# Half of x and grad_out turned by DMA, gate sums on VectorE, and quartered group loads in a gated spectral and dense kernel

## The chip, the cores and the metric

The kernel runs on one core of one Trainium2 chip. A core has a matrix engine (TensorE, PE in the profile, with its weight loads as PEld), a vector engine (VectorE, DVE), a scalar engine (ScalarE, ACT), a general engine (GpSimd, POOL) and a sync engine (SyncE, SP). In this kernel SP and POOL hand out the DMA transfers, each in the order of its own queue. SBUF is the memory on the core that the engines read, PSUM is where TensorE writes, DRAM is the chip's main memory. The metric is the time on the device from the first to the last instruction, in microseconds (us).

## The reference

The function mixes two branches with a gate per row and is differentiated; the kernel computes the output and the eight gradients.

```python
x = A_x                                          # (1, 2048, 1024), bf16
g = sigmoid((x * gate_w).sum(-1, keepdims=True))
a = irfft2(rfft2(x) * (w_r + 1j * w_i))          # spectral branch
h = relu(x_B @ w1 + b1) ** 2                     # dense branch, F = 3584
b = h @ w2 + b2
out = g * a + (1 - g) * b
# and the vector-Jacobian product with grad_out for
# A_x, w_r, w_i, w1, b1, w2, b2, gate_w
```

In the reference's `_fwd_reference` the dense branch reads the same `x` as the spectral branch.

## The kernel before

The 2048 rows are cut into 16 tiles of 128 rows (`NT`), the 1024 columns into 8 chunks of 128 (`DC`), and F = 3584 into 28 chunks of 128 (`FC`). Everything is written as Python generators, and `spread` (L948) interleaves a main generator with a side one, some side steps to each main step. A planner in the framework then sets the order on each engine from the order of the code and the data; each engine runs its own list in order.

The stages are:

- The opening (L976 to L1029). `rows_of_x` loads x tiles into `xsrc` buffers (four of them), `rows_of_grad` loads grad_out tiles into `dbn`. `turn_x` and `turn_grad` turn a tile on PE: eight 128x128 transposes into PSUM by `turn_tile` (L571 to L576), and one copy into `xT` (by ScalarE) or `dbT` (by VectorE). `gate` (L584) computes the gate of four tiles: 32 matmuls with one column each, two sigmoids into `omg` (1 - g) and `gcol` (g), and a scaling of the four `dbn` tiles by `omg` on VectorE (L597). A turn of a `dbn` tile comes after its scaling.
- `mlp_in` (L635) does the dense branch's first half. `hidden` (`forth`) multiplies two chunks of `w1` by `xT` (`ph`, eight matmuls of 512 columns) and takes relu and square on ScalarE; `grads` (`back_`) multiplies `w2T` by `dbT` (`pd`, eight matmuls) and ends in `dhT` on VectorE (L661). `ph` and `pd` share two PSUM banks. A step covers 512 rows (`s`, four row tiles) and one chunk of F. For the first two pairs of chunks (`fp` 0 and 1, here called a block of F each) the steps go through `s` from 0 to 3, forth for both, back for both; the other 12 run one by one. `load_w1` loads a `w1` pair, and `load_w2` loads `w2T` by two DMAs that transpose. `finish` stores `h2T` and `dhT` to DRAM through POOL.
- The side work of that stage is the first Fourier stage of x and then of grad_out (`first_stage_of_x`, `first_stage_of_grad`): `folds` on VectorE, `row_stage` and `first_columns` on PE, and stores of `z` through POOL. Its input tiles are the `src` buffers, loaded through SP.
- `mlp_grads` (L743) computes the gradients of w2 and w1 in 14 jobs. Each job needs a group: 512 columns of `h2T` or `dhT`, brought back from DRAM by four transposing DMAs on SP (`group`, L749). There are two group buffers, and the next job's group is asked for at the start of a job. The side work is the middle of the Fourier work (`fft_mid`) and its last part (`fft_out`), which also loads `r` tiles through SP and stores through POOL.
- `mlp_out` (L827) computes the output and the gradient of x.

Of the kernel before, what the change touches and what calls it, by code (L numbers as in the profile page):

```python
# [10 lines left out]
P = 128  # L11
BF16 = mybir.dt.bfloat16
# [113 lines left out]
def kernel(  # L126
# [66 lines left out]
    gwcol = cols("gwcol", [DC], BF16)  # L193
# [279 lines left out]
    def fft_out():  # L473
# [64 lines left out]
        load(0), load(1)  # L538
        folded(0)
        for n in range(len(tiles) + 1):  # L540
            if n < len(tiles):
                rows_back(n)
                yield
            if n > 0:
                columns_back(n - 1)
            if n + 2 < len(tiles):
                load(n + 2)
            if n + 1 < len(tiles):
                folded(n + 1)
            yield  # L550
# [15 lines left out]
    def source(i, view, earlier=None, tag="src"):  # L566
        src = f1.tile([P, D], BF16, name=tag, tag=tag, bufs=4)
        after(ld(out=src[:], in_=view[i]), earlier)
        return src
# [8 lines left out]
    def vectors(vrow):  # L578
        vps = tps.tile([P, FC + DC], BF16, name="vps", tag="tr", bufs=2)
        nc.tensor.transpose(vps[:], vrow[:], identb[: FC + DC, : FC + DC])  # L580
        nc.vector.tensor_copy(out=b1col[:], in_=vps[:, 0:FC])
        nc.vector.tensor_copy(out=gwcol[:], in_=vps[:, FC : FC + DC])

    def gate(i0):  # L584

        c_ = slice(i0, i0 + 4)
        pg = tps.tile([P, 4], FP32, name="pg", tag="tr", bufs=2)
        for i in range(i0, i0 + 4):
            for dc in range(DC):
                mm(  # L590
                    pg[:, i - i0 : i - i0 + 1], lhsT=xT[:, dc, of_tile(i)], rhs=gwcol[:, dc : dc + 1],
                    start=(dc == 0), stop=(dc == DC - 1), skip_group_check=True,
                )
        nc.scalar.activation(omg[:, c_], pg[:], ACT.Sigmoid, scale=-1.0)
        nc.scalar.activation(gcol[:, c_], pg[:], ACT.Sigmoid)
        for i in range(i0, i0 + 4):
            nc.vector.tensor_scalar(out=dbn[:, i, :], in0=dbn[:, i, :], scalar1=omg[:, i : i + 1], scalar2=None, op0=ALU.mult)  # L597

    def first_stage_of_x():
        f, ft = {0: folds(f1, xs[0], later["last"])}, {}  # L600
        for i in range(NT + 1):
            if i + 3 < NT:
                xs[i + 3] = source(i + 3, x_perm, later["last"])
            if i < NT:
                ft[i] = row_stage(f1, f[i], kf[:], later["last"])
                yield
            if i > 0:
                first_columns(f1, cf, 0, i - 1, ft[i - 1], later["last"])
            if i + 1 < NT:
                f[i + 1] = folds(f1, xs[i + 1], later["last"])  # L610
            yield
# [23 lines left out]
    def mlp_in():  # L635
# [38 lines left out]
        wide = lambda n_: wb.tile([P, 2, 2 * SW], BF16, name=n_, tag=n_, bufs=4)  # L674
        rows_ = lambda s: slice(s * SW, (s + 1) * SW)

        def load_w1(fp):
            w1[fp] = wb.tile([P, DC, PW], BF16, name="w1g", tag="w1g", bufs=3)
            ld(out=w1[fp][:], in_=w1v[:, :, fp * PW : (fp + 1) * PW])
# [6 lines left out]
        def back_(fp, s, c):  # L686
            fg, pr = divmod(fp, NPR)
            step = 2 * s + c
            last = grads(2 * fp + c, s, rows_(s), rTs.pop((fp, s, c)), dh[fp, s // 2][:, c, rows_(s % 2)])
            later["last"] = last  # L690
            if 8 * pr + step == 3:
                later["blocks"] = last
                if 0 < fg < FG - 1:
                    load_w2(fg + 1, last)
            if c == 1 and s % 2 == 1:
                finish(fp, s // 2)
# [14 lines left out]
        for s in range(4):  # L711
            for what in (forth, back_):
                for fp in range(2):
                    for c in range(2):
                        what(fp, s, c)
                        yield
            if s == 2:
                load_w1(2)
                load_w2(1, later["last"])
        for fp in range(2, FC // 2):  # L720
            if fp + 1 < FC // 2:
                load_w1(fp + 1)
            for s in range(4):
                for c in range(2):
                    forth(fp, s, c)
                    back_(fp, s, c)
                    yield
# [15 lines left out]
    def mlp_grads():  # L743
# [5 lines left out]
        def group(scr, fg, earlier=None):  # L749
            t_ = strm.tile([P, NT, FGW], BF16, name="grp", tag="strm", bufs=2)  # L750
            v_ = scr[:].rearrange("c p s -> (c p) s")[fg * FGW : (fg + 1) * FGW, :]
            for k in range(4):
                after(turned(t_[:, 4 * k : 4 * (k + 1), :], v_[:, 4 * k * P : 4 * (k + 1) * P]), earlier)
            return t_
# [3 lines left out]
        nxt = group(*jobs[0], later["blocks"])  # L758
# [3 lines left out]
        for n, (scr, fg) in enumerate(jobs):  # L762
            cur = nxt
            if n + 1 == len(jobs):
                later["block"] = blocks(h2T_scr)(0)
            else:
                nxt = group(*jobs[n + 1], later["blocks"])
# [12 lines left out]
            if scr is h2T_scr:  # L780
                for fb_ in range(FGC):
                    wo = wb.tile([P, D], BF16, name="wo2", tag="wo2", bufs=2)
                    for hf in range(NH):
# [6 lines left out]
                        last = nc.scalar.copy(out=wo[:, hf * H : (hf + 1) * H], in_=pw[:])  # L790
                        if n in (2, 3):
# [6 lines left out]
            else:  # L798
                for d_ in range(DC):
# [7 lines left out]
                    nc.scalar.copy(out=wo[:], in_=pw[:])  # L807
# [168 lines left out]
    zeros = f1.tile([P, H], BF16, name="zeros", tag="zeros")  # L976
    nc.vector.memset(zeros[:], 0.0)
    pz = tps.tile([P, H], FP32, name="pz", tag="tr", bufs=2)
    for _ in range(7):
        mm(pz[:], lhsT=zeros[:, 0:P], rhs=zeros[:], start=True, stop=True)  # L980
# [3 lines left out]
    vrow = f1.tile([FC + DC, P], BF16, name="vrow", tag="vrow")  # L984
    st(out=vrow[0:FC, :], in_=B_b1.rearrange("(fc p) -> fc p", p=P))
    st(out=vrow[FC : FC + DC, :], in_=gate_w.rearrange("(fc p) -> fc p", p=P))
# [3 lines left out]
    for i in range(4):  # L990
        turn_x(i)
    vectors(vrow)
# [4 lines left out]
    stage = None  # L997
    for k in range(NT // 4):
        i = 4 * k
        if k + 1 < NT // 4:  # L1000
            rows_of_grad(k + 1)
        next(units)
        turn_grad(i), turn_grad(i + 1)
        next(units)
        turn_grad(i + 2)
        next(units)
        turn_grad(i + 3)
        next(units)
        if stage:
            next(stage)  # L1010
        next(units)
        if k + 1 < NT // 4:
            turn_x(i + 4), turn_x(i + 5)
        next(units)
        if k + 1 < NT // 4:
            turn_x(i + 6), turn_x(i + 7)
        next(units)
        if k + 1 < NT // 4:
            gate(4 * (k + 1))
        if k + 2 < NT // 4:  # L1020
            rows_of_x(k + 2)
        if k == 0:
            for n in range(3):
                xs[n] = source(n, x_perm)
            stage = first_stage_of_x()
        next(stage)
        next(units)
        next(stage)
# [6 lines left out]
    n = 0  # L1035
    mixed = spread(units, first, 0.9)
    while n < 72:
        next(mixed)
        n += 1
# [13 lines left out]
    todo = 1 + 12 * (S2 // 2) + 2 * NT  # L1053
# [41 lines left out]
```

## Time and profile before

The times of the kernel before:

| what | value |
|---|---|
| median of 3 timed runs | 1309.12 us |
| lowest, highest | 1309.04 us, 1311.78 us |
| span of the profiled execution | 1308.4 us |
| DMA traffic over the span | 234.20 MB, 179 GB/s in the mean |

The profile is one execution. A line of the groups reads: code line, engine, operation, what is written `<-` what is read, shapes, count, then busy time and mean duration of one, then the idle time of the engine just before them and what ended most of it. A line of the timeline reads: start, duration, engine, line, operation, and a count where neighbours are merged. A line of the waits reads: who waited `<-` for whom, total, times, longest. In windows over the span PE's share stands close to full from 12 us on:

| window, us | PE busy | DVE busy | ACT busy | DMA share |
|---|---|---|---|---|
| 0 to 12 | 8.20 | 0.59 | 6.31 | 0.85 |
| 12 to 60 | 47.14 | 25.61 | 29.11 | 0.81 |
| 60 to 444 | 381.62 | 146.20 | 207.34 | 0.52 |
| 444 to 850 | 402.33 | 266.62 | 125.39 | 0.85 |
| 850 to 900 | 47.35 | 21.87 | 21.93 | 0.55 |
| 900 to 1309 | 402.50 | 221.72 | 34.45 | 0.66 |

The DMA share is the mean busy share of 16 DMA engines in the window.

### The profile page before, as it was taken

To read this page: it belongs to the slowest core of one execution; us is meant where nothing else is said; L and a number is where in the kernel's file an instruction comes from. 1 tells how busy PE (TensorE), PEld (TensorE's weight loads), DVE (VectorE), ACT (ScalarE), POOL (GpSimd) and SP (SyncE) were. 2 spreads that over 40 slices of the span, in tenths; PEclk is the share of its full clock that TensorE was granted. 3 is DMA by queue.
4 is the path that set the end of the run, shared out by engine and by line. 5 is a ranking of instruction groups with operands and counts; after the bars stand their busy time and mean duration, and the time that the engine had idled before them with its cause. 6 is when DMAs were issued, how large, how long until landed. Compare 5 with 4: busy or idle time off the path is not lost. (4 is left out here: it accounts for less than half of the span.)

```text
span 1308.4 us, 18055 instructions
## 1 busy us (share of the span) xinstructions
PE 1289.1 (99%) x6922; PEld 627.4 (48%) x7057; DVE 682.6 (52%) x1516; ACT 424.5 (32%) x722; POOL 191.3 (15%) x337
## 2 busy tenths in 40 slices
PE   8999999999999999999999999999999999999998
PEld 5555544555544444444444445554444444444443
DVE  3554424444312495677766772445767678722222
ACT  5656655666533323323233333342111111000000
POOL 0111111111110122122113221221000001000000
PEclk9999999999999999999999999999999999999999
DMA  9566354554526688898797759956999986743440
GB/s 298 181 185 178 129 155 144 184 142 157 146 97 161 173 217 183 240 242 197 185 178 159 156 140 272 306 193 175 224 198 216 228 202 195 215 130 105 131 119 25
DMA packets 314280, 234.20 MB, mean 179 GB/s; under 512 B 183701, under 2 KB 263601, under 8 KB 314193
## 3 DMA queue, kind: packets, MB, share of 16 engines
q1 hardware_dynamic: 289552, 150.58, 48.7%
q0 software_dynamic: 24640, 82.46, 19.0%
q8 instruction: 55, 0.90, 0.3%
q14 instruction: 33, 0.26, 0.1%
HBM read 107.14 MB, written 81.81 MB: 144 GB/s over the span
## 5 line engine op out<-in xcount | busy, mean ns | idle before, releaser
L647 PE MATMUL ph<-xT,w1g 128*128 128x512 bf16 x862 | 217.0, 379 | 1.7
L657 PE MATMUL pd<-dbT,w2T 128*128 128x512 bf16 x879 | 209.9, 379 | 1.1
L802 PE MATMUL pw<-grp,res 128*128 128x512 bf16 x872 | 200.0, 379 | 1.9 <-ACT wo L807 0.7
L786 PE MATMUL pw<-dbn,grp 128*128 128x512 bf16 x875 | 199.6, 379 | 1.1
L872 PE MATMUL acc<-w,hblk 128*128 128x512 bf16 x875 | 195.7, 379 | 1.1
L661 DVE SCALAR_TENSOR_TENSOR dhT<-pd,rT 128x512 bf16<-128x512 f32 x112 | 77.4, 691 | 228.6 <-PE pd L657 170.2
L932 PE MATMUL accg<-w1Tr,hblk 128*128 128x512 bf16 x878 | 192.9, 379 | 0.9
L932 PEld LDWEIGHTS <-hblk 128*128 128x128 bf16 x896 | 87.4, 98 | 105.7 <-issue 0.9
L657 PEld LDWEIGHTS <-w2T 128*128 128x128 bf16 x896 | 87.2, 98 | 102.5
L786 PEld LDWEIGHTS <-grp 128*128 128x128 bf16 x896 | 86.8, 98 | 103.2 <-issue 0.9
L872 PEld LDWEIGHTS <-hblk 128*128 128x128 bf16 x896 | 86.3, 98 | 98.5
L802 PEld LDWEIGHTS <-res 128*128 128x128 bf16 x896 | 86.2, 98 | 98.6 <-issue 1.0
L647 PEld LDWEIGHTS <-w1g 128*128 128x128 bf16 x896 | 84.7, 98 | 89.1
L649 ACT ACTIVATE rT<-ph,b1col 128x512 bf16<-128x512 f32 x112 | 76.9, 686 | 111.2 <-PE ph L647 107.9
L936 DVE TENSOR_TENSOR gxo<-accg,g 128x512 bf16<-128x512 f32 x32 | 22.1, 690 | 120.9 <-PE accg L932 120.9
L790 ACT CAST wo<-pw 128x512 bf16<-128x512 f32 x56 | 32.7, 584 | 142.1 <-PE pw L786 136.0
L807 ACT CAST wo<-pw 128x512 bf16<-128x512 f32 x56 | 32.8, 585 | 136.6 <-PE pw L802 78.4
L650 ACT ACTIVATE h2T<-rT 128x512 bf16<-128x512 bf16 x112 | 70.5, 629 | 2.5
L505 ACT CAST rt<-pki 128x1024 f16<-128x1024 f32 x32 | 32.6, 1018 | 98.1 <-PE pki L503 98.0
L331 DVE TENSOR_TENSOR x<-px,common 128x1024 f16<-128x1024 f32 x32 | 38.8, 1220 | 40.7 <-ACT common L328 40.7
L532 POOL DMA_DIRECT2D ax_scr<-yo x32 | 17.3, 540 | 235.4 <-DVE yo L531 223.9
L873 DVE SCALAR_TENSOR_TENSOR ot<-acc,omg,af 128x512 bf16<-128x512 f32 x32 | 23.9, 747 | 52.8 <-PE acc L872 52.7
(182 smaller groups left out, 1300.8 us busy)
## 6 DMA issues: line engine op xcount, KB each, us to landing
h2T_scr<-h2T POOLq DMA_DIRECT2D x28, 512.0 KB, 4.2
dhT_scr<-dhT POOLq DMA_DIRECT2D x28, 512.0 KB, 4.9
hblk<-h2T_scr SPq DMA_DIRECT2D x8, 1792.0 KB, 8.6
hblk<-dhT_scr SPq DMA_DIRECT2D x8, 1792.0 KB, 8.5
z_scr<-u POOLq DMA_DIRECT2D x32, 256.0 KB, 2.9
z<-z_scr SPq DMA_DIRECT2D x16, 512.0 KB, 4.9
y_scr<-pc POOLq DMA_DIRECT2D x16, 512.0 KB, 7.5
r<-y_scr SPq DMA_DIRECT2D x32, 256.0 KB, 3.8
```

The source lines that it names most:

```text
L331: V(out=x[:, j, :, 0:H].rearrange("p c (i g) -> p c i g", g=4), in0=px[:].rearrange("p c (g i) -> p c i g", g=4), in1=common[:].rearrange( ...
L647: mm(ph[:], lhsT=w1g[:, dc, fc % 2 * P : (fc % 2 + 1) * P], rhs=xT[:, dc, ss], start=(dc == 0), stop=(dc == DC - 1))
L649: nc.scalar.activation(rT[:], ph[:], ACT.Relu, bias=b1col[:, fc : fc + 1])
L650: nc.scalar.activation(h2T, rT[:], ACT.Square)
L657: mm(pd[:], lhsT=w_[:, ec, fc % FGC * P : (fc % FGC + 1) * P], rhs=dbT[:, ec, ss], start=(ec == 0), stop=(ec == DC - 1),)
L661: return STT(out=dhT, in0=pd[:], scalar=2.0, in1=rT[:], op0=ALU.mult, op1=ALU.mult, accum_out=gb1part[:, fc, sb : sb + 1],)
L786: mm(pw[:], lhsT=cur[:, t, fb_ * P : (fb_ + 1) * P], rhs=dbn[:, t, hf * H : (hf + 1) * H], start=(t == 0), stop=(t == NT - 1),)
L790: last = nc.scalar.copy(out=wo[:, hf * H : (hf + 1) * H], in_=pw[:])
L802: mm(pw[:], lhsT=xr[t][:, d_ * P : (d_ + 1) * P], rhs=cur[:, t, :], start=(t == 0), stop=(t == NT - 1),)
L807: nc.scalar.copy(out=wo[:], in_=pw[:])
L872: turn["PE"] = mm(acc[:], lhsT=cur[:, fc, t2 * P : (t2 + 1) * P], rhs=w2[:, fc, cs], start=(fc == 0), stop=(fc == FC - 1))
L932: turn["PE"] = mm(acc[:], lhsT=cur[:, fc, t2 * P : (t2 + 1) * P], rhs=w1T[:, fc, cs], start=(fc == 0), stop=(fc == FC - 1),)
```

## The change

It has five parts.

1. The gate's dot products move from PE to VectorE. `gate_dot(i)` multiplies a row tile of x by `gate_w`, which is broadcast to all 128 partitions by a load through POOL, and sums along the row into `gdot`. `gate` takes its sigmoids from there. The gate's part of `vectors` goes.
2. x and grad_out tiles 8 to 15 are turned by transposing DMAs on SP, x from DRAM and grad_out from the scaled `dbn` in SBUF. Tiles 0 to 7 are still turned on PE. All 16 row tiles of x are still loaded, for the gate.
3. The opening of `mlp_in` takes four blocks of F (`fp` 0 to 3) where it took two: both halves of the blocks with `s` 0 and 1 first, then with 2 and 3. `w1` gets four buffers instead of three, `dhT` three instead of four, and the loads of `w1` and `w2T` move with this. The first Fourier stage of x starts later, and its loads go through POOL.
4. In `mlp_grads`, the four DMAs of a group are asked for one at a time, after four of the eight steps of a job.
5. Smaller edits: the warm-up of PE takes 25 matmuls of 128 columns instead of 7 of 512; a sigmoid of one column at the start loads ScalarE's table; `fft_out` has three more yields before its first steps, and `todo` counts them.

```diff
@@ fft_out @@
         load(0), load(1)
+        yield
+        yield
         folded(0)
+        yield
@@ opening helpers @@
+    def gate_dot(i):
+        junk = f1.tile([P, D], BF16, name="junk", tag="zeros")
+        nc.vector.tensor_tensor_reduce(
+            out=junk[:], in0=rows[i][:], in1=gw_bc[:], scale=1.0, scalar=0.0,
+            op0=ALU.mult, op1=ALU.add, accum_out=gdot[:, i : i + 1],
+        )
     def gate(i0):
         c_ = slice(i0, i0 + 4)
-        pg = tps.tile([P, 4], FP32, name="pg", tag="tr", bufs=2)
-        for i in range(i0, i0 + 4):
-            for dc in range(DC):
-                mm(
-                    pg[:, i - i0 : i - i0 + 1], lhsT=xT[:, dc, of_tile(i)], rhs=gwcol[:, dc : dc + 1],
-                    start=(dc == 0), stop=(dc == DC - 1), skip_group_check=True,
-                )
-        nc.scalar.activation(omg[:, c_], pg[:], ACT.Sigmoid, scale=-1.0)
-        nc.scalar.activation(gcol[:, c_], pg[:], ACT.Sigmoid)
+        nc.scalar.activation(omg[:, c_], gdot[:, c_], ACT.Sigmoid, scale=-1.0)
+        nc.scalar.activation(gcol[:, c_], gdot[:, c_], ACT.Sigmoid)
@@ first_stage_of_x @@
-                xs[i + 3] = source(i + 3, x_perm, later["last"])
+                xs[i + 3] = source(i + 3, x_perm, later["last"], load=st)
@@ mlp_in @@
-        wide = lambda n_: wb.tile([P, 2, 2 * SW], BF16, name=n_, tag=n_, bufs=4)
+        wide = lambda n_: wb.tile([P, 2, 2 * SW], BF16, name=n_, tag=n_, bufs=4 if n_ == "h2T" else 3)
-            w1[fp] = wb.tile([P, DC, PW], BF16, name="w1g", tag="w1g", bufs=3)
+            w1[fp] = wb.tile([P, DC, PW], BF16, name="w1g", tag="w1g", bufs=4)
-                if 0 < fg < FG - 1:
+                if 1 < fg < FG - 1:
                     load_w2(fg + 1, last)
-        for s in range(4):
+        parts = [(0, 0), (1, 0), (0, 2), (1, 2), (2, 0), (3, 0), (2, 2), (3, 2)]
+        for n, (s, fp0) in enumerate(parts):
+            if n == 1:
+                load_w1(2), load_w1(3)
+                load_w2(1, later["last"])
+            if n == 6:
+                load_w1(4)
+                load_w2(2, later["last"])
             for what in (forth, back_):
-                for fp in range(2):
+                for fp in (fp0, fp0 + 1):
                     for c in range(2):
                         what(fp, s, c)
                         yield
-            if s == 2:
-                load_w1(2)
-                load_w2(1, later["last"])
-        for fp in range(2, FC // 2):
+        for fp in range(4, FC // 2):
@@ mlp_grads @@
-            for k in range(4):
-                after(turned(t_[:, 4 * k : 4 * (k + 1), :], v_[:, 4 * k * P : 4 * (k + 1) * P]), earlier)
-            return t_
+            def quarter(k, earlier):
+                after(turned(t_[:, 4 * k : 4 * (k + 1), :], v_[:, 4 * k * P : 4 * (k + 1) * P]), earlier)
+            return t_, quarter
...
+                nxt, quarter = group(*jobs[n + 1])
+                if n == 0:
+                    for k in range(4):
+                        quarter(k, later["blocks"])
+            quarters = {0: 0, 1: 1, 3: 2, 4: 3} if 0 < n < len(jobs) - 1 else {}
...
                         last = nc.scalar.copy(out=wo[:, hf * H : (hf + 1) * H], in_=pw[:])
+                        if 2 * fb_ + hf in quarters:
+                            quarter(quarters[2 * fb_ + hf], last)
...
+                    last = nc.scalar.copy(out=wo[:], in_=pw[:])
+                    if d_ in quarters:
+                        quarter(quarters[d_], last)
@@ the opening @@
-    for _ in range(7):
-        mm(pz[:], lhsT=zeros[:, 0:P], rhs=zeros[:], start=True, stop=True)
+    nc.scalar.activation(gdot[:, 0:1], zeros[:, 0:1], ACT.Sigmoid)
+    for _ in range(25):
+        mm(pz[:, 0:P], lhsT=zeros[:, 0:P], rhs=zeros[:, 0:P], start=True, stop=True)
...
+    gw_bc = f1.tile([P, D], BF16, name="gw_bc", tag="gw_bc")
+    st(out=gw_bc[:], in_=gate_w.partition_broadcast(P))
...
     for i in range(4):
+        gate_dot(i)
         turn_x(i)
...
+    for k in range(2):
...
+        gate_dot(i + 4), gate_dot(i + 5)
+        if k == 0:
             turn_x(i + 4), turn_x(i + 5)
...
+    rows_of_grad(3)
+    for i in range(8, 12):
+        turned(xT[:, :, of_tile(i)], x_perm[i])
+    for i in range(8, 12):
+        turned(dbT[:, :, of_tile(i)], dbn[:, i, :])
+    for n in range(3):
+        xs[n] = source(n, x_perm, later["last"], load=st)
+    stage = first_stage_of_x()
+    for n in range(4):
+        gate_dot(12 + n)
+        next(units)
+    gate(12)
+    for i in range(12, 16):
+        turned(xT[:, :, of_tile(i)], x_perm[i])
+    for i in range(12, 16):
+        turned(dbT[:, :, of_tile(i)], dbn[:, i, :])
...
-    mixed = spread(units, first, 0.9)
+    for _ in spread((next(units) for _ in range(36)), first, 0.5):
+        pass
+    for _ in spread((next(units) for _ in range(60)), first, 0.95):
+        pass
```

In the prediction a unit is one step of `mlp_in` that the opening takes from its generator: eight `ph` or eight `pd` matmuls while forth and back are apart.

## The prediction

> **What bounds the kernel now.** I read the page's busy shares first, then TensorE's (PE's) waits, then the groups by shape, then the timeline of the opening.
>
> ```profile
> PE 1289.1 (99%) x6922; PEld 627.4 (48%) x7057; DVE 682.6 (52%) x1516; ACT 424.5 (32%) x722; POOL 191.3 (15%) x337
> ...
> PE 34%; issue 0%; DVE 0%; ACT 0%
> ```
>
> PE is busy 99% of the span, and the chain that ended last is PE alone. A microsecond leaves the span only if PE does less, or waits less. Its waits, the longest first, are few:
>
> ```profile
> PE pui L282 <- ACT e L513: 2.3, 1, 2.3
> PE pt L575 <- DMA identb<-c_identb: 1.3, 1, 1.3
> PE pz L980 <- DVE zeros L977: 1.2, 1, 1.2
> PE pw L802 <- ACT wo L807: 0.7, 1, 0.7
> ```
>
> The second and third are the start of the kernel. The first and fourth fall together, near 847 and 853 us, while SP hands out a whole turned group (last fence below). So the waits that can be won add up to 3.0 us; the rest must come from PE's own work:
>
> ```profile
> L575 PE MATMUL pt<-identb,xsrc 128*128 128x128 bf16 x128 | 9.7, 236 | 1.6 <-DMA identb<-c_identb 1.3 <-ACT xT L576 0.2
> L575 PE MATMUL pt<-identb,dbn 128*128 128x128 bf16 x128 | 9.1, 219 | 0.0
> L590 PE MATMUL pg<-gwcol,xT 128*128 128x1 bf16 x128 | 3.8, 163 | 0.3 <-DVE gwcol L582 0.3
> ```
>
> The means (219 and 163 ns) are latencies of pipelined instructions, not prices. Prices come from distances between starts. The chain in order of time gives undisturbed runs:
>
> ```profile
> 857.52 0.45 PE pki L503 x8
> 857.96 3.45 PE pw L802 x16
> ```
>
> 16 wide matmuls take 3.45 us, so 8 take 1.725. The timeline of the opening then shows what stands between two such eights:
>
> ```profile
> 13.90 1.89 PE L647 MATMUL ph<-xT,w1g 128*128 128x512 bf16 x8
> ...
> 15.63 0.61 PE L575 MATMUL pt<-identb,dbn 128*128 128x128 bf16 x8
> ...
> 16.08 1.89 PE L647 MATMUL ph<-xT,w1g 128*128 128x512 bf16 x8
> ...
> 25.22 1.89 PE L657 MATMUL pd<-dbT,w2T 128*128 128x512 bf16 x7
> ...
> 26.94 0.94 PE L590 MATMUL pg<-gwcol,xT 128*128 128x1 bf16 x32
> ...
> 27.75 1.89 PE L657 MATMUL pd<-dbT,w2T 128*128 128x512 bf16 x8
> ```
>
> From 13.90 to 16.08 is 2.18: 1.725 plus 0.455 for one turned tile. From 25.22 to 27.75 is 2.53: 0.80 for one gate of 32 tiny matmuls.
>
> **What the Trainium skill says.** "VectorE: DVE Perf Modes", The three transpose paths: a 128x128 turn costs 390 ns on TensorE, 1309 ns by DMA. The trace has 0.455 us for eight on PE in a stream, far less. "Advanced Engine Details and Errata", X-Bar Transpose (TRN2): such DMAs run about as fast as ordinary ones. No turn of one tile is in this trace; the nearest is half a w2T load, 256 rows, which is two tiles. "DMA: Bandwidth & Descriptors", Issuing engines are not separate DMA queues: moving a load from SP to POOL saves only issue time. The trace shows nothing against it. "ScalarE: Activation LUTs", What ACT_TABLE_LOAD costs: about 1.28 us plus a drain; the trace has two loads of 1.28 us, at 0.72 and 10.83.
>
> **The change, part by part.**
>
> Turning. PE keeps x and grad_out tiles 0 to 7 and drops 8 to 15: 16 tiles x 0.455 = 7.3 us off PE. The 16 PSUM copies that go with them (ACT 1.0, DVE 0.69 each) were beside PE and are worth nothing.
>
> Gates. The later three gates leave PE: 3 x 0.80 = 2.4 us. The first one stood between the last turned tile and the first wide matmul (11.50). That matmul now needs only the last xT copy, which ended at 10.81; I put it at 11.1, so 0.4 less (bounds 0.7 less to 0.3 more, as w1g(0) shares the DMAs with the new 256 KB broadcast). The warm-up, the early sigmoid and its table load are over before identb lands at 5.7: nothing, hidden behind that load.
>
> Gate dots on DVE. The nearest row is the same operation with float32 input: L850, 128x1024, 1219 ns. I take 1.3 us with its accumulator read; 16 are 21 us on an engine that was 53% busy from 12 to 60 us. The price is not the work but the place. DVE runs in order, and in the built order the dots stand ahead of what PE waits for:
> - Dots 0 to 3 wait for the gate row's broadcast. Issued near 2.5, and with the cf load's 6.8 us to landing, that gives about 8.9; four dots and one b1col copy end at 14.4, the scaled first dbn tile is there at 15.3. PE has run two eights by 14.4: 0.9 us of wait. The first relu queues behind the two sigmoids, no more than that.
> - Dot 4 stands ahead of the copy of dbT tile 3, which the first pd needs. Tile 4's load leaves SP at 17.2 and landed 3.2 later, at 20.4; dot and copy end at 22.5, PE is ready at 21.1: 1.5.
> - Dots 6 to 9 stand ahead of the dhT reads that free the two ph/pd banks: 0.8, and 0.35 for a late dbT tile 7.
> - Dots 12 and 13 stand ahead of the first dhT of block (1,0), and their rows stand on SP behind w1(2), w1(3) and the two halves of w2T(1), which wait for DVE themselves (about 33.5). SP is then free near 38, rows land near 42 to 43; dots and dhT end at 45.3 where PE is ready at 44.1: 1.3, then three times 0.3.
> Sum: 0.9 + 1.5 + 0.8 + 0.35 + 1.3 + 0.9 = 5.75, say 6. Bounds: 1, if the loads land a microsecond or two sooner and DVE catches up; 13, if the w2T halves hold SP as long as the first pair did (10.16 us) and each late dot is passed on whole.
>
> Turned loads on SP.
>
> ```profile
> 6.93 10.16 SPq L166 DMA_TRANSPOSE w2T<-in_B_w_dram  x2
> 17.21 1.93 SPq L568 DMA_DIRECT2D xsrc<-in_A_x_dram  x4
> ...
> 70.44 3.83 SPq L166 DMA_TRANSPOSE w2T<-in_B_w_dram  x2
> ...
> 830.09 15.79 SPq L166 DMA_TRANSPOSE grp<-dhT_scr  x4
> ```
>
> A pair of halves, four tiles' worth, held SP 10.2 us while the DMAs were full and 3.8 when not, so a tile takes 1 to 2.5 us of SP; I take 1.5, 24 us for 16, from about 42 on. First need: xT 8 to 11 at unit 33, near 49 + 16 x 1.725 + some first-stage work = 78; the last (dbT 12 to 15) near 101. Hidden, with 59 us for 16 turns. The first-stage x loads go from SP to POOL's queue, past the h2T, dhT and z stores; POOL was 11% busy in the opening (3.4 of 48 us), so nothing. Four blocks of F instead of two give these turns their time; the same eights run in another order: nothing on PE. dhT with three buffers: the fourth tile in use comes 8 units (over 14 us) after the store of the first, which lands in 4.9: nothing.
>
> Quartered groups. SP no longer gives 15.8 us to one group while the r loads and stores wait; I take both waits near 850 as gone, 3.0 us (bounds 0 and 3.4). The last quarter is issued after five eighths of a job of some 33 us and landed in 6 (at most 13): hidden. The three extra yields only delay the first fold, off PE.
>
> **Sum**, against its own span: -7.3 - 2.4 - 0.4 - 3.0 + 6 = -7.1; 1308.4 to 1301.3. The three timed runs are 1309.04 to 1311.78, median 1309.12, 0.7 above the span: forecast 1302.
>
> **Rivals.**
> - The dots' waits are mostly taken up: +1 instead of +6, time 1297. For it: DVE has slack, and landings of 3 us were seen. Against: an order that can't be swapped at run time.
> - The waits grow to 13 or so, or the quarters win nothing beside them: 1309, no change to measure. For it: the DMAs were full from 2 to 40 us.
> - Slower: the one-tile turns, out of SBUF above all, are not half of a w2T half but cost SP a fixed time each. Place: SP between 42 us and unit 45. From 59 / 16 = 3.7 us each PE begins to wait. At 5 us, the last would be there at 42 + 80 = 122, 21 us late: 1302 + 21 = 1323. At the skill's 1309 ns for each of eight blocks in turn it would be worse. For it: no such turn in the trace. Against: w2T halves, two tiles each, ran at 1.9 us.
>
> **How the numbers follow.** Forecast 0.55, waits taken up 0.20, no change 0.12, late turns 0.13. The forecast's own range is 1298 to 1307 (waits 2 to 11). To hold 8 in 10 over all, I leave out most of the slow rival and some of the fast: 1295 to 1311. A difference under 0.2% (2.6 us) can't be told from none here. Faster: 0.55 x 0.95 + 0.20 = 0.72. Same: 0.03 + 0.10 = 0.13. Slower: the late turns and a little of the third case, 0.15.
>
> **What would show it.** PE's L575 groups at 64 + 64 and no L590; the PE busy sum down by about 10 at equal means; PE waits between 14 and 52 us, put down to DVE (dbT, dhT), summing to 4 to 8; no wait at 845 to 855. I am wrong if PE waits for DMA into xT or dbT after 75 us, if the opening's waits exceed 11, or if new PE waits for grp quarters appear between 445 and 850.

## The result, and the profile after

The changed kernel is slower: 1327.1 us in the median of four runs (1324.18 to 1329.72), against 1310.16 us for the kernel before beside it (1309.04 to 1311.78). The ratio is 1.0128, with a 95% interval of 1.0100 to 1.0155. The forecast was 1302 us, so the sign was wrong. The profiled execution has a span of 1322.4 us, 14.0 more than before; it is the fastest of the four, so some 3 us of the median are not in it.

The page's busy shares and its chain of waits, for the changed kernel:

```profile
PE 1284.0 (97%) x6686; PEld 619.4 (47%) x6819; DVE 699.0 (53%) x1539; ACT 414.1 (31%) x714; POOL 204.1 (15%) x353
...
PE 75%; issue 11%; DVE 6%; DMA 4%; POOL 3%; ACT 1%; SPq 0%; another core or an unknown queue 0%; POOLq 0%; DVEq 0%; ACTq 0%
```

TensorE (PE) is busy only 5 us less than before, although some 10 us of turns and gate sums left it. It now idles for 38 us instead of 19. The chain that ended last now goes back over the whole span, and a quarter of it isn't PE; before, it reached back over a third of the span, all of it PE. TensorE's waits in the changed kernel say where:

```profile
PE pw L820 <- DMA grp<-dhT_scr: 8.5, 2, 7.5
PE pd L659 <- DVE dhT L663: 5.0, 1, 5.0
...
PE pd L659 <- DVE dbT L579: 1.4, 1, 1.4
```

Two waits are large and new, and they lie in two different stages. The starts of the stages, read from the timeline as the first matmul of each, split the 14.0 us:

| start of | before | after | stage longer by |
|---|---|---|---|
| `mlp_grads`, jobs on `h2T` | 445.0 | 447.5 | 2.5 (up to here) |
| `mlp_grads`, jobs on `dhT` | 670.9 | 677.0 | 3.6 |
| `mlp_out` | 897.7 | 912.4 | 8.6 |
| end | 1308.4 | 1322.4 | -0.7 |

The prediction had -4.1 for the first row (all but the quarters) and -3.0 for the second and third. Both were wrong.

**The late quarter.** The timeline of SP's queue in one job on `dhT` of the changed kernel (the job ran from 805.4 to 837.3 us), with the wait of the next job on PE:

```profile
809.66 9.49 SPq L166 DMA_TRANSPOSE grp<-dhT_scr  x1
819.26 0.51 SPq L488 DMA_DIRECT2D r<-y_scr  x1
819.83 0.42 SPq L536 DMA_DIRECT2D w<-in_B_w_dram  x1
820.34 7.04 SPq L166 DMA_TRANSPOSE grp<-dhT_scr  x1
...
830.26 6.88 SPq L166 DMA_TRANSPOSE grp<-dhT_scr  x1
...
837.86 3.61 SPq L166 DMA_TRANSPOSE grp<-dhT_scr  x1
```
```profile
847.52 1.87 PE L820 MATMUL pw<-grp,res 128*128 128x512 bf16 x4 [7.55 <-DMA grp<-dhT_scr]
```

The last quarter of the group was due near 825.8, when ScalarE's copy of the fifth step ends. It is handed out at 837.86, after the job that should have hidden it has ended, and it lands 9.6 us later. The three quarters before it held SP 9.5, 7.0 and 6.9 us; the four together make 27.0. Before the change the whole group handed out at 830.09 held it 15.8. After the wait TensorE isn't at full speed; windows of the changed kernel (us, PE busy with its instructions, granted clock, DMA share, GB/s):

```profile
840.00:844.00 4.00, 0.00 (x0) 0.78 1.03 193
844.00:848.00 4.00, 0.48 (x2) 0.50 1.03 263
848.00:852.00 4.00, 4.00 (x23) 0.50 0.32 113
852.00:853.00 1.00, 1.00 (x5) 0.77 0.98 258
```

The granted clock fell to 0.50 while PE idled and stayed there for over 4 us of work. Up to 844 PE had nothing to do. From 844 to 852 it was busy 4.48 us at half speed, which is 2.2 us lost on top of the wait, if PE's pace goes with the granted clock; the microsecond that follows, at 0.77, makes it 2.5.

**The late rows.** The timeline of the opening of the changed kernel, first SP's queue, then VectorE and PE:

```profile
34.34 8.34 SPq L166 DMA_TRANSPOSE w2T<-in_B_w_dram  x2
42.73 2.04 SPq L571 DMA_DIRECT2D xsrc<-in_A_x_dram  x4
44.82 2.96 SPq L987 DMA_DIRECT2D dbn<-in_grad_out_dram  x4
47.82 9.12 SPq L166 DMA_TRANSPOSE xT<-in_A_x_dram  x4
```
```profile
46.72 1.23 DVE L588 CUSTOM_DVE_ANT_0 junk<-xsrc,gw_bc 128x1024 bf16<-128x1024 bf16 x1 [6.08 <-DMA xsrc<-in_A_x_dram]
...
49.88 1.88 PE L659 MATMUL pd<-dbT,w2T 128*128 128x512 bf16 x5 [4.95 <-DVE dhT L663]
```

The two halves of w2T(1) hold SP for 8.34 us, so the x rows of tiles 12 to 15 leave it at 42.73. VectorE sits on the dot of tile 12 for 6.08 us, with the `dhT` that frees PE's bank queued behind it. PE waits 4.95 us, and then works at a clock of 0.50 to 0.67 until 54 us:

```profile
50.00:51.00 1.00, 1.00 (x4) 0.67 1.04 401
51.00:53.00 2.00, 1.78 (x5) 0.50 1.24 219
53.00:54.00 1.00, 1.00 (x5) 0.63 1.28 287
```

Counted as above, that is 0.33 + 0.89 + 0.37 = 1.6 us more. From 12 to 60 us PE is busy 39.5 us, where it was 47.1.

### The profile page after: what moved, and what is told of

It reads as the page before. It is cut to its first block, busy times and chain, and to the rows that moved or that the text cites. A ratio compares the mean times of both kernels' runs of the same rounds, so it can differ in the third digit from the quotient of the medians.

```text
span 1322.4 us, 17648 instructions
## 1 busy us (share of the span) xinstructions
PE 1284.0 (97%) x6686; PEld 619.4 (47%) x6819; DVE 699.0 (53%) x1539; ACT 414.1 (31%) x714; POOL 204.1 (15%) x353
## 4 chain that ended last, share of the span: by engine, by line
PE 75%; issue 11%; DVE 6%; DMA 4%; POOL 3%; ACT 1%; SPq 0%; another core or an unknown queue 0%; POOLq 0%; DVEq 0%; ACTq 0%
PE accg L952 15%; PE pd L659 13%; PE acc L892 13%; PE ph L649 13%; PE pw L802 10%; PE pw L820 5%; POOL out_dram L828 1%; DMA grp<-dhT_scr 1%; PE pu L282 1%; PE pk L249 1%; DMA src<-in_A_x_dram 1%; DVE t L450 1%; DVE t L449 1%; PE pui L282 1%; DMA b_bc<-in_B_b_dram 1%
## 5 line engine op out<-in xcount | busy, mean ns | idle before, releaser
L649 PE MATMUL ph<-xT,w1g 128*128 128x512 bf16 x870 | 214.3, 379 | 2.5 <-DMA w1g<-in_B_w_dram 1.3
L704 POOL DMA_DIRECT2D h2T_scr<-h2T x28 | 20.2, 723 | 201.0 <-ACT h2T L652 189.0
L512 ACT CAST e<-pui 128x512 f16<-128x512 f32 x32 | 18.8, 587 | 102.2 <-PE pui L282 83.4
```

The costliest lines, as they stand in the source:

```text
L649: mm(ph[:], lhsT=w1g[:, dc, fc % 2 * P : (fc % 2 + 1) * P], rhs=xT[:, dc, ss], start=(dc == 0), stop=(dc == DC - 1))
```

## The experiments

Each run is timed beside the kernel before on the same chip. The last column is where `mlp_in` ends and how long the two halves of `mlp_grads` take in the profiled execution.

| version | median, us | ratio to before, 95% | `mlp_in` to / `h2T` half / `dhT` half |
|---|---|---|---|
| before | 1310.0 | 1 | 445.0 / 225.9 / 226.8 |
| after | 1327.1 | 1.0128 [1.0100, 1.0155] | 447.5 / 229.5 / 235.4 |
| whole_groups | 1313.8 | 1.0031 [1.0018, 1.0044] | 448.0 / 227.9 / 224.4 |
| quarters_alone | 1312.6 | 1.0020 [1.0011, 1.0030] | 447.3 / 226.0 / 230.5 |
| quarters_early | 1326.0 | 1.0130 [1.0115, 1.0146] | 447.8 / 227.9 / 237.7 |
| quarters_no_yields | 1326.7 | 1.0119 [1.0087, 1.0150] | 454.3 / 228.5 / 234.2 |
| yields_alone | 1309.6 | 0.9995 [0.9986, 1.0004] | 446.5 / 227.8 / 225.4 |
| no_dots | 1326.4 | 1.0123 [1.0087, 1.0159] | 449.5 / 229.0 / 239.2 |
| dots_alone | 1316.0 | 1.0049 [1.0035, 1.0062] | 451.6 / 225.9 / 225.4 |
| rows_early | 1332.7 | 1.0168 [1.0148, 1.0189] | 453.6 / 230.2 / 236.8 |
| rows_early2 | 1308.6 | 0.9988 [0.9978, 0.9999] | 443.7 / 227.8 / 225.1 |
| pe_turns | 1320.1 | 1.0079 [1.0063, 1.0095] | 453.7 / 227.9 / 225.8 |
| rows_early2_warm | 1318.8 | 1.0070 [1.0055, 1.0084] | 453.8 / 228.1 / 228.9 |

The row "before" is the median of the 36 runs beside whole_groups, quarters_alone, rows_early and no_dots; beside the others it was 1309.7 to 1310.2. The last column is one execution for each version, and it holds a difference that no edit made: before and after ran their first wide matmuls at full pace (7 in 1.67 us, 15 in 3.63), and all other versions ran theirs slower (8 in 3.57 in quarters_alone, 16 in 6.03 in whole_groups). quarters_alone and yields_alone don't touch the opening, and `mlp_in` ends 2.3 and 1.5 us later in them. So some 2 us of the first figure are chance. no_dots has two runs only. The order on each engine is set by a planner from the code, so an edit in the opening can also swap neighbours that it doesn't name. Where that decided something, it is told below.

### Undoing the quarters: whole_groups

```diff
                 nxt, quarter = group(*jobs[n + 1])
-                if n == 0:
-                    for k in range(4):
-                        quarter(k, later["blocks"])
-            quarters = {0: 0, 1: 1, 3: 2, 4: 3} if 0 < n < len(jobs) - 1 else {}
+                for k in range(4):
+                    quarter(k, later["blocks"])
+            quarters = {}
```

> The changed kernel with the four DMAs of a group asked for together at the start of a job, as before. Theory (the pacing hands the last quarter of the last group out too late, and PE waits 7.5 us and then runs at half clock for 4 us): no PE wait on grp near 840; the dh half of the gradient jobs takes 226 to 229 us instead of 235.4; the span 1322.4 - 10.4 + 3.0 = 1315. Rival (the late group comes from the shifted side work and the w2 loads, not from the pacing): the wait stays, span 1322 to 1327.

The quarters cost 13.3 us in the changed kernel (1327.1 less 1313.8; 12.6 in the two halves of `mlp_grads` in the profiled executions), and everything else in the change together costs 0.3%. SP's queue in this version, at the same place:

```profile
803.15 17.44 SPq L166 DMA_TRANSPOSE grp<-dhT_scr  x4
...
835.17 12.24 SPq L166 DMA_TRANSPOSE grp<-dhT_scr  x4
```

All four DMAs of a group go at the start of a job, the `dhT` half takes 224.4 us, and the two old waits near 850 don't come back. So those did not need quarters to go.

### The quarters in the kernel before: quarters_alone

The edit is part 4 of the change, put into the kernel before, and nothing else.

> The kernel before with only the quartered groups. Theory of the late quarter: slower than before by some 7 us (about 1316), with a PE wait on a grp load of several us late in the dh half. Rival, the prediction's: both waits near 850 go and nothing comes in their place, 1306.

```profile
PE pki L503 <- DMA r<-y_scr: 4.0, 1, 4.0
```

The line is from TensorE's waits. The old waits (2.3 and 0.7) are gone and one of 4.0 for an `r` load stands in their place, near 799 us: two quarters hold SP 8.0 us from 785.8 on, and the first `r` tiles leave behind them, at 795.2, where they left at 787.0 before. The time is 0.2% longer. The quarters gain nothing, then, not even by themselves.

How long SP was held by the 48 transposing group DMAs that start between 444 and 905 us, one execution for each version. Each DMA counts with its own time; a merged line of the timeline won't do, as it can take in pauses between its DMAs.

| version | SP held, us | per DMA, us | longest, us |
|---|---|---|---|
| before | 154 | 3.2 | 8.2 |
| whole_groups | 139 | 2.9 | 8.4 |
| yields_alone | 140 | 2.9 | 7.2 |
| quarters_alone | 155 | 3.2 | 9.4 |
| quarters_early | 161 | 3.4 | 10.1 |
| quarters_no_yields | 172 | 3.6 | 9.6 |
| after | 184 | 3.8 | 12.2 |

In the changed kernel the same DMAs, with the same bytes, hold the queue 45 us longer when they are handed out one by one among loads and stores (184 against 139). In the kernel before they don't (155 against 154), and the quarters still gain nothing there. So a longer hold adds to the loss but isn't needed for one: what stands behind a quarter, and how late a quarter leaves, is enough.

### When the quarters are due: quarters_early

```diff
-            quarters = {0: 0, 1: 1, 3: 2, 4: 3} if 0 < n < len(jobs) - 1 else {}
+            quarters = {0: (0, 1), 1: (2, 3)} if 0 < n < len(jobs) - 1 else {}
```

Each of the two steps then asks for both of its quarters.

> The changed kernel with the quarters asked for two at a time, after the first and the second step of a job. Theory: what cost the dh half its time was the due time of the last quarter (after the fifth step, 32.5 us into a job of 33), not the cutting in four. In the job that ran from 805 to 837 the four requests then leave SP at about 810, 818, 826 and 833 and land by 838 to 840: TensorE's wait for a group near 840 falls from 8.5 to below 2, the stretch at half clock after it goes, and the time is 1312 to 1318 (1327 less most of the 13 that whole groups won). Rival A, the cutting itself: requests with stores and other loads between them on SP cost the same wherever they are due; a wait of 6 or more for a group stays and the time is 1324 to 1329. Rival B, the collision only moves: no wait for a group, but one of 4 or more for r or another load near 850, and 1318 to 1324.

SP's queue and PE in this version:

```profile
789.20 10.12 SPq L166 DMA_TRANSPOSE grp<-dhT_scr  x1
...
801.05 1.28 SPq L488 DMA_DIRECT2D r<-y_scr  x3
```
```profile
804.53 0.62 PE L503 MATMUL pki<-ki,r 128*128 128x128 f16 x4 [9.75 <-DMA r<-y_scr]
```

My theory fell: 1326.0 us, no gain. (Its "32.5 us into a job" is when the last quarter left SP; it was due some 20 us into the job.) The wait for a group near 840 did go, as expected, but a wait of 9.75 us for `r` took its place at another point: rival B in kind, with a time in rival A's range. A transposing DMA held SP for 10.1 us, and this time the first loads of the last Fourier part stood behind it. So an earlier due time of the last quarter doesn't by itself bring the loss back. In both timings something that PE needs soon left SP late behind a transposing DMA, and the due times picked what it was; no third timing was run.

### The yields: yields_alone and quarters_no_yields

The first puts the three yields and their count (part 5) into the kernel before; the second takes them out of the changed kernel:

```diff
         load(0), load(1)
-        yield
-        yield
         folded(0)
-        yield
...
-    todo = 4 + 12 * (S2 // 2) + 2 * NT
+    todo = 1 + 12 * (S2 // 2) + 2 * NT
```

> The kernel before with only the three more yields ahead of the last Fourier part and todo counting them. Theory (with whole groups in the changed kernel the two waits near 850 were gone without quarters, so the shift of the side work removes them): dh half of the gradient jobs 223.5 us instead of 226.8, time about 1306.5. Rival (they went for another reason, or come and go): no change, 1310.

> The changed kernel without its three extra yields at the start of the last Fourier part (and without their count in todo). Quarters alone cost the kernel before 3 us; undoing them in the changed kernel won 13. Theory, an interaction: the yields shift the last Fourier part by some 3 side steps, so that its five loads (8.8 us held at the longest) stand on SP just ahead of the last quarter of that one job; without the yields the last quarter leaves SP before them or lands in time, the wait for a group near 840 falls below 2 and a wait for r of about 4 comes in its place, as it did with quarters alone; time 1314 to 1320. Rival: the yields have no part in it (they made no difference alone); the wait of 8 and the half clock stay, 1325 to 1329, and the 10 us between the two are from the later opening, which shifts the jobs against the side work.

The yields alone make no measurable difference: 0.9995, its interval reaching over 1. In the profile the `dhT` half is 1.4 us shorter and the `h2T` half 1.9 longer, and the old waits near 850 are gone, which is what the changed kernel's quarters had been given credit for in the prediction. New waits of TensorE stand in their place: 1.4 us for `y` in seven, 0.6 for `r` and 0.6 for `rf`, which is 2.6 of the 3.0 that went. Taken out of the changed kernel, the yields make no difference that shows: 1326.7 against 1327.1. TensorE's waits of quarters_no_yields:

```profile
PE pki L503 <- DMA r<-y_scr: 3.6, 1, 3.6
PE pw L817 <- DMA grp<-dhT_scr: 3.3, 1, 3.3
PE pw L799 <- DMA grp<-h2T_scr: 2.5, 1, 2.5
```

The wait for a group near 840 is gone and one of 3.6 for `r` has come, as the theory said. But group waits of 3.3 (near 690 us) and 2.5 have come with it, and the time didn't follow. This run isn't a clean one for the yields: its opening ends 6.8 us later than the changed kernel's in the profiled execution (454.3 and 447.5), which the edit doesn't name, and the two halves of `mlp_grads` are 2.2 us shorter (462.7 and 464.9).

From 485 us on, SP's list in this version is the same, line for line, as in quarters_alone, which had only the first of the three waits. So the same order cost 3.8 us in the two halves there (456.5 against 452.7 before) and 10.0 here. Why the quarters are so much dearer after the new opening is not settled. That each group lands with no time to spare, so that a small shift of PE against the DMAs decides whether it waits, would fit, and the four runs of this version spread from 1318 to 1329; but no run separates it.

### The dots: no_dots and dots_alone

no_dots leaves the products out (`gdot` is a copy of a column of `gw_bc`, so the gates and all that hangs on them are other numbers) and keeps every load:

```diff
-        nc.vector.tensor_tensor_reduce(
-            out=junk[:], in0=rows[i][:], in1=gw_bc[:], scale=1.0, scalar=0.0,
-            op0=ALU.mult, op1=ALU.add, accum_out=gdot[:, i : i + 1],
-        )
+        nc.vector.tensor_scalar(out=gdot[:, i : i + 1], in0=gw_bc[:, 0:1], scalar1=1.0, scalar2=None, op0=ALU.mult)
```

> The changed kernel with the 16 gate dot products left out (each replaced by a copy of one column, so the gates are not the reference's); rows and turned loads stay. Theory (the opening's waits come from the dots' place on DVE): the waits on dbn, dbT and dhT go, mlp_in ends near 438, span about 1313. Rival (the extra DMA traffic of rows and turned tiles makes them): at most 3 us off, mlp_in ends at 444 or later.

The wait for `dhT` near 50 us stays, at 6.7 us, though no dot stands ahead of it. VectorE in this version:

```profile
52.21 0.49 DVE L595 TENSOR_SCALAR dbn<-dbn,omg 128x1024 bf16<-128x1024 bf16 x1 [7.53 <-DMA dbn<-in_grad_out_dram]
```

It now sits on the scaling of a grad_out row, which leaves SP even later than the x rows. So at this place the work of the dots isn't the cause; the rows are late.

dots_alone puts part 1 (dots, broadcast, sigmoids) into the kernel before, with its warm-up and with all tiles turned on PE.

> The kernel before with only the gate dots on VectorE. Theory (from the run without dots: the dots by themselves hardly hold PE): the 2.4 us of gates on PE and 0.4 at the first are saved, less at most 1 of waits, time about 1307.5. The prediction's reading (dots ahead of dbT copies and dhT reads cost about 1 us each time): nothing is left of the saving, 1310 or more.

My theory for this one fell: dots alone make the kernel slower, by 0.5%, though they take some 3 us of gate sums off PE. VectorE, PE, in order of time:

```profile
23.99 1.23 DVE L585 CUSTOM_DVE_ANT_0 junk<-xsrc,gw_bc 128x1024 bf16<-128x1024 bf16 x1 [2.80 <-DMA xsrc<-in_A_x_dram]
...
26.41 0.69 DVE L576 COPY dbT<-pt 128x1024 bf16<-128x1024 bf16 x1
...
27.24 1.02 PE L656 MATMUL pd<-dbT,w2T 128*128 128x512 bf16 x4 [2.77 <-DMA dbn<-in_grad_out_dram]
```

The copy of a `dbT` tile, from data long in PSUM, waits behind two dots (the second follows at 25.26), and the first of these waits for an x row. PE needs that copy. (The trace's label names a DMA for PE's 2.77 us; the copy ended at 27.1, just before PE went on, and so it is the likelier releaser.) This is the prediction's second dot step, seen without the rest of the change. It isn't all of the loss: TensorE also waits 1.8 us for `w1g`, 2.0 for `f` and 1.6 for a scaled `dbn` tile in this opening, and idles 15.0 us in it against 7.0 before.

### The order on SP: rows_early and rows_early2

Both hand out the rows of tiles 12 to 15 before w2T(1). rows_early keeps the quarters and asks for w2T(1) late, so that it fell behind eight turned loads; rows_early2 puts it directly after the rows, and has whole groups:

```diff
                 load_w1(2), load_w1(3)
-                load_w2(1, later["last"])
+                early = later["last"]
...
+                        if n == 1 and what is back_ and fp == 1 and c == 1:
+                            load_w2(1, early)
...
         rows_of_x(k + 2)
+        if k == 1:
+            rows_of_grad(3)
         next(units)
...
-    rows_of_grad(3)
```

> The changed kernel with the loads of rows 12 to 15 of x and grad_out placed on SP ahead of the two halves of w2T(1). Theory (dots 12 and 13 stand ahead of dhT on DVE and wait for rows that stand behind w2T(1) on SP): the PE wait of 4.95 us on dhT near 45 to 50 us and the half clock after it go, mlp_in ends near 441 instead of 447.5, span about 1316. Rival (the DMAs are too full, so the rows are as late or w2T(1) is late in their place): mlp_in ends at 446 or later, with a wait on w2T or on the rows.

> The changed kernel with whole groups, and on SP the order rows 12 to 15 of x and grad_out, then w2T(1), then the turned tiles. Theory (late rows, not the dots' own work, hold DVE and so PE; SP's order decides who is late): no wait on dhT near 45 to 52 us and none on w2T, mlp_in ends near 441 instead of 448.0 with whole groups, time about 1307. Rival (the DMAs are full, whatever the order): a wait of 5 us or more on w2T, rows or w1, mlp_in ends at 446 or later, 1313.

TensorE's longest waits of rows_early (but for one on `grp`, 9.8 in two), then of rows_early2:

```profile
PE pd L659 <- DMA w2T<-in_B_w_dram: 9.7, 1, 9.7
```
```profile
PE pd L659 <- DVE dbT L579: 3.1, 2, 1.7
PE ph L649 <- DMA w1g<-in_B_w_dram: 2.1, 1, 2.1
```

In rows_early the `dhT` wait went, and a wait of 9.7 us for w2T came: eight turned loads held SP from 41.0 to 62.3 us ahead of it. With the order rows, w2T(1), turned loads, neither is left. rows_early2 takes 1308.6 us, 5.2 less than whole_groups and the fastest version here. Its ratio of 0.9988 [0.9978, 0.9999] is under 1, but by less than the 0.2% that I set as the bound for a difference.

### What turning on DMA is worth: pe_turns

Whole groups, and all 32 tiles turned on PE, without any turned load:

```diff
-    for i in range(8, 12):
-        turned(xT[:, :, of_tile(i)], x_perm[i])
-    for i in range(8, 12):
-        turned(dbT[:, :, of_tile(i)], dbn[:, i, :])
...
+        turn_grad(8 + n)
...
+    for n in range(4):
+        turn_x(12 + n)
+        next(units)
+    for n in range(4):
+        turn_grad(12 + n)
+        next(units)
```

> The changed kernel with whole groups and all 32 tiles turned on PE, no turned loads; everything else, four blocks and dots, stays. Theory (the turned loads come after the waits and save PE their 7.3 us): mlp_in ends near 455, time about 1321. Rival (the turned loads fill the DMAs and cost the opening what they save): mlp_in ends at 449 or sooner, 1314.

Against whole_groups `mlp_in` ends 5.7 us later (453.7 and 448.0), and the medians differ by 6.4. So the turned loads win most of what the prediction gave them, 7.3 us.

### The clock at the start: rows_early2_warm

rows_early2 with `range(48)` in place of `range(25)` for the warm-up matmuls.

> The version with whole groups and the rows of tiles 12 to 15 ahead of w2T(1), which took 0.9988 of the time before, with 48 warm-up matmuls of 128 columns in place of 25. Theory: the first ph matmuls (12 to 18 us) run at half clock in some executions because TensorE is idle between the last warm-up matmul and the first turned tile; with warm-up until the first tile is there, the first 16 ph matmuls take 3.6 us and not 6, and the median falls by 1 to 2.5: 1306 to 1307.5, 0.9965 to 0.998 of the time before. Rival: the clock at the start is not set by the warm-up, or the later end of the warm-up pushes the turned tiles back by as much: 1308 to 1310, 0.998 to 1.000.

PE and VectorE in this version:

```profile
25.34 0.61 PE L578 MATMUL pt<-identb,dbn 128*128 128x128 bf16 x8 [3.94 <-DVE dbT L579]
```
```profile
23.45 1.23 DVE L588 CUSTOM_DVE_ANT_0 junk<-xsrc,gw_bc 128x1024 bf16<-128x1024 bf16 x1 [5.45 <-DMA xsrc<-in_A_x_dram]
```

The warm-up now runs into the first turned tile (its last matmul ends at 6.11 us; with 25 it was 3.86), but the first `ph` matmuls start at 11.51 and take 5.31 us for 16, as in rows_early2 (15 in 5.31 there; 3.63 in the changed kernel's execution). So in this execution more warm-up didn't bring the full pace. The time rose by 10 us for other reasons: with 23 more matmuls the planner put a dot ahead of two `dbT` copies and split the loads of rows on SP differently, the dot stood 5.45 us on its row, and PE waited 3.94. A wait of 4.60 us for `f`, at 72.3 us, is new as well. What the warm-up itself is worth is left open. The run shows once more that in this opening one row's place on SP, with an in-order VectorE behind it, is worth several microseconds.

## Why the prediction was wrong

**Turning (-7.3): right in kind, a little less in size.** PE's groups at L578 went from 128 + 128 to 64 + 64 and the loads were hidden; pe_turns gives 5.7 to 6.4.

**Gates (-2.4 and -0.4): the first right, the second half so.** L590 is gone. The first `ph` started at 11.31, 0.2 earlier than before. It waited 1.27 us for `w1g`, which landed at 11.26 (9.24 before), and not for the last `xT` copy; the step's bounds had named that load. In most of the other versions with dots it started later than before, at 11.5 to 12.2.

**Dots 0 to 5 (0.9 + 1.5): right in place and size.** The changed kernel waits 1.00 for `dbn` at 15.9 and 1.45 for `dbT` at 24.4. For the second, tile 4's row and PE both came some 2 us later than put, so its size is in part luck. A dot took 1.22 us and 0.08 for its accumulator, as priced. A wait of 0.7 for an x row at 22.3 was not foreseen; between 25 and 44 us, where 1.15 was expected, no wait shows.

**Rows 12 to 15 (1.3 + 0.9): right place, wrong size.** The step that failed is "SP is then free near 38": w2T(1) held SP 8.34 us and not some 4.5, so rows left at 42.7 and the first of the four dots began at 46.7. PE waited 4.95 and lost 1.6 to the clock, for which the sum had no term. The bound for this case, 13 in all, named the cause; I took the middle.

**Sum of the opening.** Up to the first gradient matmul PE idles 16.8 us, 7.0 before, so the waits make 9.8 where 6 were put; 7.6 of them lie between 12 and 60 us. PE is busy 7.3 us less, and that holds 1.6 for the clock, so some 8.9 of work went, where some 10 were priced. That is the +2.5 of the trace; the forecast had -4.1. Waits and clock are the larger part of the miss.

**Turned loads (1.5 us of SP each): mechanism right, size off.** The four lots held SP 9.12, 13.91, 9.66 and 13.86 us, which is 46.6 for 16 turns, 2.9 each; the slower rival began at 3.7. PE never waited for them in the changed kernel. The Trainium skill's "Advanced Engine Details and Errata", X-Bar Transpose (TRN2), cited in the prediction, has such DMAs run as fast as regular ones. This trace doesn't agree. A tile out of `dbn` held the queue 3.5 us in the mean, one out of DRAM 2.3, and a plain x row 0.5 (2.04 for four). From leaving SP to landing it took 7.1 to 13.7 us out of `dbn` and 3.6 to 7.8 out of DRAM, against 3.9 to 5.9 for the x rows just before.

**First-stage loads on POOL (nothing): nearly.** One wait of 0.9 us at 72.4, behind a `src` tile that came late. (POOL's 3.4 of 48 us are 7% busy, not 11%.)

**Quarters (-3.0, bounds 0 and 3.4): the step that decided, and the wrong sign.** Two sentences failed. "SP no longer gives 15.8 us to one group while the r loads and stores wait": the parts gave SP no relief. The four quarters near 810 to 841 us held it 27.0, and over the stage the parts hold it longer than whole groups do in this kernel, 184 us against 139. "The last quarter is issued after five eighths of a job ... hidden" took the time of the request for the time of its leaving: SP hands out in order, the three quarters before it held it 23.4 us, and it left 12 us after it was due. PE then waited 7.5 us for it and lost 2.5 to the clock. whole_groups puts the cost of all quarters at 13.3 us. The bounds had nothing below zero, although the prediction's own fence showed four such DMAs holding SP 15.8 us; that a queue which hands out in order would pass each hold on to what stands behind it was a reason to keep a loss in the range.

**The rivals.** The slower one, late turns, fell. The second came nearest, with 9.8 us more of idle PE in the opening and quarters that win nothing; but that the quarters lose was in none of them. The signs listed at the end of the prediction were good: the clause on "new PE waits for grp quarters" is what came true.

**Yields (nothing): right**, shown by yields_alone. The two waits near 850 that I gave to the quarters go with the yields alone, and 3.0 us of time don't go with them, since 2.6 us of new waits come.

Of the 3.6 us in the `h2T` half, about 2 come with the yields (1.9 in yields_alone, 2.0 in whole_groups), which give them back in the `dhT` half; that leaves 1.6 with the quarters.

## What to carry to other kernels

A queue that hands out in order turns every slow request into a wait for what is behind it: before cutting a transfer into parts, ask when the last part can leave, not when it is requested, and look at what PE needs next behind each. The parts can also hold the queue longer together than the whole did (184 us against 139 in the changed kernel), though they need not (155 against 154 in the kernel before). The same holds for an engine in order: a cheap operation that waits for a late load is as dear as that load, so move loads first and work second. When a wait ends, add what the clock takes afterwards.

## What was not expected of the hardware

- Transposing DMAs of equal size held SP's queue anything from 1.3 to 12.2 us each in the gradient stage of the changed kernel, 3.8 in the mean; handed out in fours (whole_groups) it was 2.9. In the kernel before the mean was 3.2 either way.
- While turned loads run, few bytes move though the DMA engines are busy: in rows_early2 the window from 60 to 100 us has a DMA share of 1.18 at 205 GB/s, and 840 to 844 us in the changed kernel 1.03 at 193, where 790 to 795 moved 406 at 1.06. What else ran in these windows isn't separated.
- The prices of a wait and of its aftermath: 4.95 us of idle PE brought a half clock until 4 us after the restart, worth 1.6 us; 7.55 us brought one until 5 us after, worth 2.5.
- The first wide matmuls of the kernel took 3.63 us for 15 in one execution and 5.31 for 15 or 6.03 for 16 in others, which moves the end of the opening by some 2 us from one execution to the next. The granted clock of the profile doesn't always show it: it reads 0.51 to 0.63 from 12 to 16 us in rows_early2, and 1.00 in whole_groups, which took 6.03. No run here tells what sets it.
